# Reordering the end of an expert search, and starting the next search right behind the first index

## The chip, the cores and the metric

One core of a Trainium2 chip. The metric is the device time of one execution in microseconds (us). Engines: PE (TensorE, matmuls and transposes), DVE (VectorE), ACT (ScalarE), POOL (GpSimd), SP (SyncE, which issues DMAs).

## The reference

Causal attention over q, k, v of shape (4, 12, 448, 64), then a mixture of experts over its 1792 output rows of 768 numbers. Each of eight experts takes exactly 224 rows:

```python
logits = x @ w_gate
order = np.argsort(-logits.flatten())
for idx in order:
    tok, e = idx // E, idx % E
    if assigned[tok] >= 0 or counts[e] >= cap:
        continue
    assigned[tok] = e
    counts[e] += 1
for e in range(E):
    h = np.maximum(x[assigned == e] @ w1[e], 0.0)
    out[assigned == e] = h @ w2[e]
```

So the expert that fills up first keeps its 224 best rows; its logits and those rows are then struck out, and the rest goes on.

## The kernel before

**Attention** takes about the first 136 us; its rows go to a table in DRAM (tile xd), the logits stay in tile L: 128 partitions, NB = 14 blocks of tokens, E = 8 experts.

**Searches.** Class Router finds, one after the other, which expert fills up next and which rows it takes. Search p has these steps, each a generator in which `yield "DVE", 0.75` means: what follows runs on DVE, and the planner books 0.75 us for it.

- best (lines 891 to 899; search 0 has early and first in its place): the best logit m, its expert tm and a one-hot A of each row, then integer keys.
- round (901 to 930), five times: compare the keys with thresholds (same, line 824, tile G, on DVE), count them per expert with 14 matmuls (line 929), and pick (932 to 946) a threshold from the counts.
- close (948 to 960): DVE operations most, cw, tx (which expert), then two cuts of the keys. In their midst expert (962 to 964) writes the expert's number ei as an integer, which SP reads to load that expert's weights.
- members (975 to 1018): gq and a scan on DVE (983, 987), two matmuls (990, 991), then pos, slot and val (994 to 998), and one-hots oh of the slots, eight blocks and then six (1004; blocks go in pairs, so slices 0:4 and 4:7); the second half of val (1008) stands between them. Fourteen matmuls (1013) make the index of the rows, a DVE cast (1017) writes it as idx.
- retire (1020 to 1030): cm and acc, which hold minus 1e30 for the expert and for the rows that are gone, are added to L.

**Experts.** For search p's rows: POOL issues two indirect DMAs (gather, line 1336, halves u = 0 and 1) that fetch 112 rows each from xd; PE turns them (1357), ACT copies them (1364), and the first product with w1 follows (first, 1399 for the first half of expert 0, 1403 and 1404 later), then w2 (1432, 1433, 1464). Weights are loaded in eight pieces of 768 KB by SP (fetch, 1312 and 1315); pieces 1 to 3 of expert 0 wait for a copy of ei (ei2, 1340) that POOL makes behind the second gather. The large matmuls take each number as a sum of two, so ACT rounds each piece of weights (1321) and DVE subtracts (1327).

**The order of the work** on each engine is fixed when the program is built. Class Schedule (76 to 159) keeps tasks with durations, priorities and latencies between engines, and always gives the engine that is free first its ready task of highest priority. The steps of a search have 10.9, the first transposes of expert 0 have 13 and the first matmuls 13.5 (1185, 1218). Booked times: gather 1.03 on POOL, then 0.85 until the DMA, 0.96 for it and 1.0 until the rows of half 0 are there (1181, 1182); a transpose step 0.2, its ACT copy 0.27 (1194, 1198). While the flag filling is set, until the first expert matmul, PE's free time is filled with matmuls that nothing reads (filler, 1345).

**What held the second search back.** route (1090 to 1113) chains the searches. After search 0 it sets `self.pace = self.sent`, an event that gather fires for half 1 of expert 0 (1343), with a latency of 1.0. On the chip itself, tile big, which the operation cm reads (1025), is only written by POOL behind the two gathers (1341). The PSUM banks pass from attention to the experts in banks (1071), called from turn (1351).

Of the kernel before, what the change touches and what calls it, by code (L numbers as in the profile page):

```python
# [7 lines left out]
F32 = mybir.dt.float32  # L8
F32R = mybir.dt.float32r
F16 = mybir.dt.float16  # L10
# [4 lines left out]
OP = mybir.AluOpType  # L15
# [4 lines left out]
C, P, NC = 112, 128, 4  # L20
E, CAP = 8, 224
DM, FF = 768, 1024
NB = 14
# [15 lines left out]
BIG = 1.0e30  # L39
# [723 lines left out]
class Router:  # L763
    def __init__(self, nc, cs, k, L):
        self.nc, self.cs, self.k, self.L = nc, cs, k, L

        self.G = cs.tile([P, NB * 128], BF, name="G")
        nc.gpsimd.memset(self.G, 0.0)
        self.oh = cs.tile([P, NB * C + 32], F16, name="oh")
        nc.gpsimd.memset(self.oh[:, NB * C:], 0.0)  # L770
        self.cds, self.turn = {}, 0
        self.big = cs.tile([P, 1], F32, name="big")
        for n in sorted({d.n for ds_ in DIGITS for d in ds_}):
            self.cds[n] = cs.tile([128, 2, E + 1], F16, name=f"cd{n}")
            nc.gpsimd.memset(self.cds[n], 0.0)
# [172 lines left out]
    def close(self):  # L948
        nc, sb, k = self.nc, self.sb, self.k
        yield "DVE", 1.0  # L950
        most = sb.tile([P, 1], F32, name="most")
        nc.vector.tensor_reduce(most, self.nn[:P, :E], axis=AX.X, op=OP.max)
        cw = sb.tile([P, E], F32, name="cw")
        nc.vector.scalar_tensor_tensor(cw, self.nn[:P, :E], most, k["w8"], op0=OP.is_equal, op1=OP.mult)
        self.tx = sb.tile([P, 1], F32, name="tx")
        nc.vector.tensor_reduce(self.tx, cw, axis=AX.X, op=OP.max)
        self.cut = sb.tile([P, 2, NB], F16, name="cut")
        nc.vector.tensor_scalar(self.cut[:, 0], self.kw, most, None, op0=OP.is_gt)
        self.expert()
        nc.vector.tensor_scalar(self.cut[:, 1], self.kw, most, None, op0=OP.is_equal)  # L960

    def expert(self):
# [3 lines left out]
    def last(self):  # L966
        nc, sb = self.nc, self.sb
        yield "DVE", 0.75
        self.m = sb.tile([P, NB], F32, name="m")
        nc.vector.tensor_reduce(self.m, self.L, axis=AX.X, op=OP.max)  # L970
        self.tx = sb.tile([P, 1], F32, name="tx")
        nc.vector.tensor_reduce(self.tx, self.wo, axis=AX.X, op=OP.max)
        self.expert()

    def members(self, last=False):
        nc, sb, k = self.nc, self.sb, self.k
        yield "DVE", 0.5
        gq = sb.tile([P, 2, NB], F16, name="gq")
        if last:
            nc.vector.tensor_scalar(gq[:, 0], self.m, -BIG / 8, None, op0=OP.is_gt)  # L980
            nc.vector.memset(gq[:, 1], 0.0)
        else:
            nc.vector.scalar_tensor_tensor(gq, self.tm[:, None, :].to_broadcast([P, 2, NB]), self.tx, self.cut,
                                           op0=OP.is_equal, op1=OP.mult)
        g2 = gq.rearrange("p s b -> p (s b)")
        run = sb.tile([P, 2 * NB], F16, name="run")
        nc.vector.tensor_tensor_scan(run, k["on"][:P, :2 * NB], g2, LIFT, op0=OP.mult, op1=OP.add)
        yield "PE", 0.06
        p = self.psum()
        nc.tensor.matmul(p[:, 0:2 * NB], k["tri"], g2, start=True, stop=False)  # L990
        nc.tensor.matmul(p[:, 0:2 * NB], k["on"], run, start=False, stop=True)
        yield "DVE", 0.4
        pos = sb.tile([P, NB], F32, name="pos")
        nc.vector.tensor_reduce(pos, p[:, 0:2 * NB].rearrange("p (s b) -> p b s", s=2), axis=AX.X, op=OP.min)
        slot = sb.tile([P, NB], F16, name="slot")
        nc.vector.scalar_tensor_tensor(slot, pos, -1.0, pos, op0=OP.mult, op1=OP.max)
        val = sb.tile([P, NB, 2], F16, name="val")
        nc.vector.scalar_tensor_tensor(val[:, :, 1], pos, 0.0, k["tv"], op0=OP.is_gt, op1=OP.mult)
        oh = self.oh
        hot = oh[:, :NB * C].rearrange("p (b t s) -> p b t s", t=C, s=2)  # L1000
        for s in (slice(0, 4), slice(4, 7)):
            yield "DVE", 0.07 + 0.117 * (s.stop - s.start)
            shape = [P, s.stop - s.start, C, 2]
            nc.vector.tensor_tensor(hot[:, s], k["io"][:, None].to_broadcast(shape),
                                    slot.rearrange("p (b s) -> p b s", s=2)[:, s, None, :].to_broadcast(shape),
                                    op=OP.is_equal)
            if s.start == 0:
                nc.vector.tensor_tensor(val[:, :, 0], k["tv"], val[:, :, 1], op=OP.subtract)
        yield "PE", 0.41
        p = self.psum()  # L1010
        for b in range(NB):
            o = b // 2 * 2 * C
            nc.tensor.matmul(p[:, 0:2], oh[:, o:o + 256].rearrange("p (t s) -> p t s", s=2)[:, :, b % 2], val[:, b],
                             start=b == 0, stop=b == NB - 1)
        yield "DVE", 0.07
        self.idx = sb.tile([C, 2], I32, name="idx", bufs=E)
        nc.vector.tensor_copy(self.idx, p[:C, 0:2])
        self.pos = pos

    def retire(self):  # L1020
        nc, sb, L = self.nc, self.sb, self.L
        b3 = [P, NB, E]
        yield "DVE", 1.05
        cm = sb.tile([P, E], F32, name="cm")
        nc.vector.tensor_scalar(cm, self.k["w8"], self.tx, self.big, op0=OP.is_equal, op1=OP.mult)
        acc = sb.tile([P, NB], F32, name="acc")
        nc.vector.tensor_scalar(acc, self.pos, float(C), -BIG, op0=OP.is_lt, op1=OP.mult)  # L1027
        nc.vector.tensor_tensor(L, L, cm[:, None, :].to_broadcast(b3), op=OP.add)
        nc.vector.tensor_tensor(L, L, acc[:, :, None].to_broadcast(b3), op=OP.add)
        nc.vector.scalar_tensor_tensor(self.wo, self.wo, self.tx, self.wo, op0=OP.not_equal, op1=OP.mult)  # L1030

class Experts(Schedule):
# [57 lines left out]
    def route(self):  # L1090
        rt = self.rt
        for p in range(E):
# [10 lines left out]
                yield from rt.close()  # L1103
            else:
                yield from rt.last()
            self.eis.append(rt.ei)
            self.fire(self.ei[p])
            yield from rt.members(p == E - 1)
            self.idx[p] = rt.idx
            self.fire(self.ix[p])  # L1110
            if p < E - 1:
                self.pace = self.sent if p == 0 else self.pace
                yield from rt.retire()

    def late(self):
        at = self.at
# [216 lines left out]
    def gather(self, p, u):  # L1333
# [4 lines left out]
        if p == 0 and u == 1:  # L1338
            self.ei2 = self.sb.tile([1, 1], I32, name="ei2")
            self.nc.gpsimd.tensor_copy(self.ei2, self.eis[0][0:1])  # L1340
            self.nc.gpsimd.memset(self.rt.big, -BIG)
            self.fire(self.again)
            self.fire(self.sent)

# [196 lines left out]
```

## Time and profile before

| what | value |
|---|---|
| median of 3 runs | 452.05 us (451.25 to 452.68) |
| the profiled execution | 450.93 us |
| its span, first to last instruction | 449.2 us |
| PE busy | 438.9 us (98%) |
| DVE busy | 368.9 us (82%) |
| ACT busy | 295.8 us (66%) |
| POOL busy | 75.1 us (17%) |
| mean granted clock of PE | 0.998 |

All times in the rows below are us from the span's start, in the one profiled execution. The 98% of PE contain the fillers, so they don't say that PE had work everywhere. A merged line such as "x14" gives the start of the first, the time from there to the end of the last, and the count. In brackets stands how long the engine had been idle before, and what released it.

### The profile page before, as it was taken

To read this page: it belongs to the slowest core of one execution; us is meant where nothing else is said; L and a number is where in the kernel's file an instruction comes from. 1 tells how busy PE (TensorE), PEld (TensorE's weight loads), DVE (VectorE), ACT (ScalarE), POOL (GpSimd) and SP (SyncE) were. 2 spreads that over 40 slices of the span, in tenths; PEclk is the share of its full clock that TensorE was granted. 3 is DMA by queue.
4 is the path that set the end of the run, shared out by engine and by line. 5 is a ranking of instruction groups with operands and counts; after the bars stand their busy time and mean duration, and the time that the engine had idled before them with its cause. 6 is when DMAs were issued, how large, how long until landed. Compare 5 with 4: busy or idle time off the path is not lost.

```text
span 449.2 us, 11897 instructions
## 1 busy us (share of the span) xinstructions
PE 438.9 (98%) x4506; PEld 380.6 (85%) x4506; DVE 368.9 (82%) x1246; ACT 295.8 (66%) x733; POOL 75.1 (17%) x192
## 2 busy tenths in 40 slices
PE   7999999999999999999999999999999999999994
PEld 4767676767678899999999999899989999999994
DVE  4998888878889579998999999899999698787400
ACT  6999999999978066556366456556554676865310
POOL 7112132312120201020111103003002500100101
PEclk9999999999999999999999999999999999999999
DMA  7994584560005877776587588378667969871201
GB/s 258 421 387 166 172 341 154 206 271 3 2 1 158 245 261 244 258 217 249 155 266 268 153 268 281 118 237 278 187 196 234 305 210 286 272 231 46 63 15 47
DMA packets 20041, 91.30 MB, mean 203 GB/s; under 512 B 2288, under 2 KB 5392, under 8 KB 18704
## 3 DMA queue, kind: packets, MB, share of 16 engines
q1 hardware_dynamic: 16896, 79.08, 52.5%
q0 software_dynamic: 2608, 11.01, 7.7%
q8 instruction: 35, 0.57, 0.5%
q10 hardware_dynamic: 480, 0.46, 0.3%
q14 instruction: 22, 0.18, 0.1%
HBM read 79.53 MB, written 11.01 MB: 202 GB/s over the span
## 4 chain that ended last, share of the span: by engine, by line
PE 67%; issue 19%; DMA 4%; DVE 4%; POOL 3%; ACT 2%; SPq 0%; POOLq 0%; ACTq 0%
PE po L1464 15%; PE s L245 9%; PE s L323 9%; PE ph L1403 9%; PE s L299 6%; PE ph L1404 4%; DMA wr<-in_w 3%; PE rt L929 2%; PE po L1432 2%; POOL out L1482 2%; PE s L253 1%; PE s L411 1%; DMA raw<-in_qk 1%; PE ph L1357 1%; PE ph L1399 1%
## 5 line engine op out<-in xcount | busy, mean ns | idle before, releaser
L1327 DVE TENSOR_TENSOR wl<-wr,wh 128x512 fp32r<-128x512 f32 x186 | 119.7, 681 | 0.0
L1403 PE MATMUL ph<-xhl,wh 128*128 128x448 f32 x336 | 109.6, 380 | 0.0
L1321 ACT CAST wh<-wr 128x1536 fp32r<-128x1536 f32 x62 | 91.8, 1482 | 18.3 <-DMA wr<-in_w 15.1
L269 ACT ACTIVATE P<-Sm,mx 128x320 f32<-128x320 f32 (+3 forms) x168 | 87.8, 538 | 6.0 <-DVE mx L262 5.5
L1404 PE MATMUL ph<-xhl,wl 128*128 128x224 f32 x336 | 89.2, 265 | 0.0
L1464 PE MATMUL po<-wh,H 128*112 128x384 f32 x320 | 85.4, 342 | 0.0
L1403 PEld LDWEIGHTS ph<-xhl,wh 128*128 128x128 f32 x336 | 63.2, 188 | 5.1 <-issue 0.3
L1404 PEld LDWEIGHTS ph<-xhl,wl 128*128 128x128 f32 x336 | 64.2, 191 | 0.0
L1464 PEld LDWEIGHTS po<-wh,H 128*112 128x112 f32 x320 | 55.0, 175 | 0.3
L1464 PE MATMUL po<-wl,H 128*112 128x384 f32 x160 | 54.7, 342 | 0.0
L245 PE MATMUL s<-raw 64*128 64x320 f32 (+2 forms) x288 | 46.9, 443 | 1.1 <-DMA raw<-in_qk 1.1
L1432 PE MATMUL po<-H,wh 128*128 128x448 f32 x144 | 46.9, 380 | 0.0
L323 PE MATMUL s<-PT,v 128*64 128x64 f32 (+3 forms) x644 | 44.5, 290 | 0.0
L323 PEld LDWEIGHTS s<-PT,v 128*64 128x64 f32 x644 | 31.0, 138 | 12.4 <-issue 8.2
L262 DVE CUSTOM_DVE_ANT_0 Sm<-s,MK 128x320 f32<-128x320 f32 (+2 forms) x72 | 33.2, 486 | 8.9 <-PE s L245 8.4
L1433 PE MATMUL po<-H,wl 128*128 128x224 f32 x144 | 38.3, 266 | 0.0
L1336 POOL DMA_INDIRECT xio<-xd,idx x16 | 17.7, 1104 | 116.8 <-DVE acc L1027 92.0
L1482 POOL DMA_INDIRECT out<-xio,idx x15 | 16.7, 1114 | 121.7 <-ACT xio L1468 62.9
L1409 ACT ACTIVATE H<-hs 128x224 fp32r<-128x224 f32 x60 | 23.4, 392 | 20.1 <-DVE hs L1417 20.0
L1413 ACT COPY hc<-ph 128x224 f32<-128x224 f32 x60 | 20.5, 341 | 23.2 <-PE ph L1404 19.3
L245 PEld LDWEIGHTS s<-raw 64*128 64x128 f32 x288 | 28.6, 187 | 7.6 <-DVE PT L305 2.9
L269 ACT ACTIVATION_READ_ACCUMULATOR P<-Sm,mx 128x1 f32 x168 | 34.6, 206 | 0.0
(212 smaller groups left out, 749.9 us busy)
## 6 DMA issues: line engine op xcount, KB each, us to landing
wr<-in_w SPq DMA_DIRECT2D x64, 768.0 KB, 5.0
raw<-in_qk SPq DMA_DIRECT2D x10, 1024.0 KB, 11.4
v<-in_v SPq DMA_DIRECT2D x11, 896.0 KB, 9.3
xd<-xio SPq DMA_DIRECT2D x2, 1152.0 KB, 5.3
raw<-in_qk SPq DMA_DIRECT2D x3, 512.0 KB, 5.9
xd<-xio SPq DMA_DIRECT2D x3, 384.0 KB, 3.7
v<-in_v SPq DMA_DIRECT2D x2, 448.0 KB, 6.6
xd<-xio SPq DMA_DIRECT2D x3, 192.0 KB, 5.1
```

What stands on the lines that cost most here:

```text
L245: self.nc.tensor.matmul(ts[sd][:, o:o + m], q[:, QS[i]:QS[i] + P], k, start=True, stop=True)
L262: self.nc.vector.tensor_tensor_reduce(Sm[:, QO[i] + sd * m:QO[i] + sd * m + m], self.S.pop((pp, sd, i)), mk, -0.125, 3.0e38, OP.add, OP.mi ...
L269: self.nc.scalar.activation(X[:, s], Sm[:, s], AF.Exp, bias=mx[:, o], scale=-1.0, accum_out=rw[:, o])
L299: self.nc.tensor.transpose(t[z][:, n * 64:n * 64 + 64], X[h, o:o + P], idf[h, h])
L323: self.nc.tensor.matmul(self.AV[pp][sd * 64:sd * 64 + 64, w:w + m], v[:, j if j < 3 else 3 + (3, 2, 0, 1)[j - 3], :], PT[:, o:o + m], star ...
L1321: self.nc.scalar.copy(hi, self.R[p, c])
L1327: self.nc.vector.tensor_sub(lo[:, s], self.R[p, c][:, s], hi[:, s].bitcast(F32))
L1403: nc.tensor.matmul(t[:, :2 * CAP], hi[:, s], x.rearrange("p z t -> p (z t)"), start=d == 0, stop=False)
L1404: nc.tensor.matmul(t[:, :CAP], lo[:, s], x[:, 0], start=False, stop=d == 5)
L1432: self.nc.tensor.matmul(t[:, :2 * CAP], hi[:, o:o + 128], H[:, f].rearrange("p z t -> p (z t)"), start=f == 0, stop=False)
L1433: self.nc.tensor.matmul(t[:, :CAP], lo[:, o:o + 128], H[:, f, 0], start=False, stop=f == 7)
L1464: self.nc.tensor.matmul(self.O[u, z][:, :384], self.H[p][:, f, h, u * C:u * C + C], w[:, o:o + 384], start=f == 0 and n == 0, stop=f == 7 ...
```

## The change

close: the first cut now stands between cw and tx, and ei is gone from there. In search 0, ei is written in members, behind the scan, while DVE would wait for PE (the argument also); in the later searches it is written behind the second cut. members: the one-hots come in ten blocks and four; the first val operation has moved behind the ten, in front of the second one; and cm and acc, which were the first two operations of retire, follow the four. The planner's 1.05 us for retire become 0.75. big is written once at the start of the program. route no longer waits for sent, and calls banks right behind the first index.

```diff
@@ -770,6 +770,7 @@
         nc.gpsimd.memset(self.oh[:, NB * C:], 0.0)
         self.cds, self.turn = {}, 0
         self.big = cs.tile([P, 1], F32, name="big")
+        nc.gpsimd.memset(self.big, -BIG)
         for n in sorted({d.n for ds_ in DIGITS for d in ds_}):
             self.cds[n] = cs.tile([128, 2, E + 1], F16, name=f"cd{n}")
             nc.gpsimd.memset(self.cds[n], 0.0)
@@ -952,11 +953,10 @@
         nc.vector.tensor_reduce(most, self.nn[:P, :E], axis=AX.X, op=OP.max)
         cw = sb.tile([P, E], F32, name="cw")
         nc.vector.scalar_tensor_tensor(cw, self.nn[:P, :E], most, k["w8"], op0=OP.is_equal, op1=OP.mult)
+        self.cut = sb.tile([P, 2, NB], F16, name="cut")
+        nc.vector.tensor_scalar(self.cut[:, 0], self.kw, most, None, op0=OP.is_gt)
         self.tx = sb.tile([P, 1], F32, name="tx")
         nc.vector.tensor_reduce(self.tx, cw, axis=AX.X, op=OP.max)
-        self.cut = sb.tile([P, 2, NB], F16, name="cut")
-        nc.vector.tensor_scalar(self.cut[:, 0], self.kw, most, None, op0=OP.is_gt)
-        self.expert()
         nc.vector.tensor_scalar(self.cut[:, 1], self.kw, most, None, op0=OP.is_equal)
 
     def expert(self):
@@ -970,9 +970,8 @@
         nc.vector.tensor_reduce(self.m, self.L, axis=AX.X, op=OP.max)
         self.tx = sb.tile([P, 1], F32, name="tx")
         nc.vector.tensor_reduce(self.tx, self.wo, axis=AX.X, op=OP.max)
-        self.expert()
-
-    def members(self, last=False):
+
+    def members(self, last=False, also=None):
         nc, sb, k = self.nc, self.sb, self.k
         yield "DVE", 0.5
         gq = sb.tile([P, 2, NB], F16, name="gq")
@@ -985,6 +984,8 @@
         g2 = gq.rearrange("p s b -> p (s b)")
         run = sb.tile([P, 2 * NB], F16, name="run")
         nc.vector.tensor_tensor_scan(run, k["on"][:P, :2 * NB], g2, LIFT, op0=OP.mult, op1=OP.add)
+        if also:
+            also()
         yield "PE", 0.06
         p = self.psum()
         nc.tensor.matmul(p[:, 0:2 * NB], k["tri"], g2, start=True, stop=False)
@@ -995,17 +996,22 @@
         slot = sb.tile([P, NB], F16, name="slot")
         nc.vector.scalar_tensor_tensor(slot, pos, -1.0, pos, op0=OP.mult, op1=OP.max)
         val = sb.tile([P, NB, 2], F16, name="val")
-        nc.vector.scalar_tensor_tensor(val[:, :, 1], pos, 0.0, k["tv"], op0=OP.is_gt, op1=OP.mult)
         oh = self.oh
         hot = oh[:, :NB * C].rearrange("p (b t s) -> p b t s", t=C, s=2)
-        for s in (slice(0, 4), slice(4, 7)):
+        for s in (slice(0, 5), slice(5, 7)):
             yield "DVE", 0.07 + 0.117 * (s.stop - s.start)
             shape = [P, s.stop - s.start, C, 2]
             nc.vector.tensor_tensor(hot[:, s], k["io"][:, None].to_broadcast(shape),
                                     slot.rearrange("p (b s) -> p b s", s=2)[:, s, None, :].to_broadcast(shape),
                                     op=OP.is_equal)
             if s.start == 0:
+                nc.vector.scalar_tensor_tensor(val[:, :, 1], pos, 0.0, k["tv"], op0=OP.is_gt, op1=OP.mult)
                 nc.vector.tensor_tensor(val[:, :, 0], k["tv"], val[:, :, 1], op=OP.subtract)
+        if not last:
+            self.cm = sb.tile([P, E], F32, name="cm")
+            nc.vector.tensor_scalar(self.cm, k["w8"], self.tx, self.big, op0=OP.is_equal, op1=OP.mult)
+            self.acc = sb.tile([P, NB], F32, name="acc")
+            nc.vector.tensor_scalar(self.acc, pos, float(C), -BIG, op0=OP.is_lt, op1=OP.mult)
         yield "PE", 0.41
         p = self.psum()
         for b in range(NB):
@@ -1020,11 +1026,8 @@
     def retire(self):
         nc, sb, L = self.nc, self.sb, self.L
         b3 = [P, NB, E]
-        yield "DVE", 1.05
-        cm = sb.tile([P, E], F32, name="cm")
-        nc.vector.tensor_scalar(cm, self.k["w8"], self.tx, self.big, op0=OP.is_equal, op1=OP.mult)
-        acc = sb.tile([P, NB], F32, name="acc")
-        nc.vector.tensor_scalar(acc, self.pos, float(C), -BIG, op0=OP.is_lt, op1=OP.mult)
+        yield "DVE", 0.75
+        cm, acc = self.cm, self.acc
         nc.vector.tensor_tensor(L, L, cm[:, None, :].to_broadcast(b3), op=OP.add)
         nc.vector.tensor_tensor(L, L, acc[:, :, None].to_broadcast(b3), op=OP.add)
         nc.vector.scalar_tensor_tensor(self.wo, self.wo, self.tx, self.wo, op0=OP.not_equal, op1=OP.mult)
@@ -1103,14 +1106,20 @@
                 yield from rt.close()
             else:
                 yield from rt.last()
-            self.eis.append(rt.ei)
-            self.fire(self.ei[p])
-            yield from rt.members(p == E - 1)
+            if p:
+                self.chosen(p)
+            yield from rt.members(p == E - 1, None if p else lambda: self.chosen(0))
             self.idx[p] = rt.idx
             self.fire(self.ix[p])
             if p < E - 1:
-                self.pace = self.sent if p == 0 else self.pace
+                if p == 0:
+                    self.banks()
                 yield from rt.retire()
+
+    def chosen(self, p):
+        self.rt.expert()
+        self.eis.append(self.rt.ei)
+        self.fire(self.ei[p])
 
     def late(self):
         at = self.at
@@ -1338,7 +1347,6 @@
         if p == 0 and u == 1:
             self.ei2 = self.sb.tile([1, 1], I32, name="ei2")
             self.nc.gpsimd.tensor_copy(self.ei2, self.eis[0][0:1])
-            self.nc.gpsimd.memset(self.rt.big, -BIG)
             self.fire(self.again)
             self.fire(self.sent)
```

## Rows read from the trace of the kernel before

**Rows 1.** Busy time by stage: stretch, length, each engine's us, PE clock, DMA share, GB/s.

```profile
156.00:170.00 14.00, 13.93 (x147) 12.97 (x146) 11.57 (x41) 9.01 (x16) 0.00 (x0) 1.00 0.71 238
```

**Rows 2.** PE's waits from 150 us on: us in total, times, longest.

```profile
PE ph L1357 <- DMA xio<-xd,idx: 0.7, 1, 0.7
PE ph L1357 <- DVE hs L1417: 0.4, 1, 0.4
PE rt L929 <- DVE G L824: 0.3, 1, 0.3
PE rt L946 <- DVE cd L943: 0.3, 1, 0.3
```

**Rows 3.** Order of time on PE, from the first index to the first expert matmuls.

```profile
150.22 0.60 PE L1013 MATMUL s<-val,oh 128*128 128x2 f16 x14
150.69 4.23 PE L1347 MATMUL s<-on 128*112 128x256 f16 x37
155.57 0.77 PE L1357 MATMUL ph<-idf,xio 112*128 112x112 f32 x6 [0.66 <-DMA xio<-xd,idx]
156.18 0.28 PE L1347 MATMUL po<-on 128*112 128x256 f16 x1
156.44 2.04 PE L1399 MATMUL po<-xhl,wr 128*128 128x112 f32 x16
```

**Rows 4.** Order of time on DVE, at the end of the first search.

```profile
147.30 0.23 DVE L954 SCALAR_TENSOR_TENSOR cw<-s,most,w 128x8 f32<-128x8 f32 x1
147.56 0.16 DVE L956 TENSOR_REDUCE tx<-cw 128x1 f32<-128x8 f32 x1
147.64 0.23 DVE L958 TENSOR_SCALAR cut<-kw,most 128x14 f16<-128x14 f32 x1
147.77 0.15 DVE L964 TENSOR_SCALAR ei<-tx 128x1 int32<-128x1 f32 x1
147.83 0.23 DVE L960 TENSOR_SCALAR cut<-kw,most 128x14 f16<-128x14 f32 x1
...
149.08 0.17 DVE L996 SCALAR_TENSOR_TENSOR slot<-pos 128x14 f16<-128x14 f32 x1
149.17 0.17 DVE L998 SCALAR_TENSOR_TENSOR val<-pos,tv 128x14 f16<-128x14 f32 x1
149.29 0.62 DVE L1004 TENSOR_TENSOR oh<-io,slot 128x896 f16<-128x896 f16 x1
149.83 0.17 DVE L1008 TENSOR_TENSOR val<-tv,val 128x14 f16<-128x14 f16 x1
149.92 0.50 DVE L1004 TENSOR_TENSOR oh<-io,slot 128x672 f16<-128x672 f16 x1
150.86 0.16 DVE L1017 CAST idx<-s 112x2 int32<-112x2 f32 x1 [0.45 <-PE s L1013]
```

**Rows 5.** Order of time on DVE, at the beginning of the second search.

```profile
154.03 0.29 DVE L1025 TENSOR_SCALAR cm<-w,tx,big 128x8 f32<-128x8 f32 x1 [3.00 <-POOL xio L1331]
...
154.35 0.28 DVE L1028 TENSOR_TENSOR L<-L,cm 128x112 f32<-128x112 f32 x1
...
157.25 1.16 DVE L824 TENSOR_TENSOR G<-kr,kk 128x1024 bf16<-128x1024 int16 x2
```

**Rows 6.** The chain that ended last: one count of a round, 14 matmuls.

```profile
163.77 0.33 PE rt L929 x14
```

**Rows 7.** Busy time by stage, columns as in rows 1, while the first weights land.

```profile
152.00:153.00 1.00, 1.00 (x11) 1.00 (x10) 0.00 (x0) 0.00 (x0) 0.69 (x2) 1.00 0.93 389
153.00:154.00 1.00, 1.00 (x12) 1.00 (x11) 0.00 (x0) 0.00 (x0) 0.99 (x4) 1.00 0.80 184
```

**Rows 8.** Order of time on POOL: three of the sixteen gathers.

```profile
151.32 1.19 POOL L1336 DMA_INDIRECT xio<-xd,idx  x1 [5.56 <-DVE idx L1017]
...
309.67 0.93 POOL L1336 DMA_INDIRECT xio<-xd,idx  x1 [29.34 <-DVE acc L1027]
...
347.06 2.94 POOL L1336 DMA_INDIRECT xio<-xd,idx  x1 [4.64 <-DVE idx L1017]
```

## The prediction

> **What bounds the kernel now.** I read three views in this order: the busy time by stage, what TensorE (PE) waited for, and the order of time on PE, VectorE (DVE) and GpSimd (POOL) around the first gather. From 156 us on, PE is the bound: in the first stage of the experts it is busy 13.93 of 14.00 us at a granted clock of 1.00 [rows 1]. Over the whole rest of the program its own waits, after the one for the first gathered rows, are three, together 1.0 us [rows 2]. So two things only can move the end: when PE's real work begins, and how much PE work lies behind that beginning.
>
> It begins like this [rows 3]. The 14 index matmuls of the first search start at 150.22. Then PE has nothing to do but 37 filler matmuls and a wait of 0.66 us, until the first gathered rows have landed at 155.57. Six transposes, one filler, and at 156.44 the first expert matmul. Between 150.8 and 155.57, PE time is free; behind 156.44 it is not.
>
> **The end of the first search** [rows 4]. The reader is to see two kinds of spacing: an operation that reads the result of the one before starts about 0.21 us after it (slot 149.08, one-hots 149.29), one that doesn't starts 0.09 to 0.13 us after it, although each lasts about 0.17 us (val 149.83, one-hots 149.92).
>
> *Closing step.* cw to tx is a dependent pair, 0.26 us apart, and the first cut takes 0.13 us of DVE (147.64 to 147.77), so put between them it fits into the wait: 0.13 us saved. The expert number ei (147.77 to 147.83) leaves the path: 0.06 us saved. I take 0.18 together. ei now runs behind the scan, where DVE waits for PE anyway. The lower bound is 0.06, if the cut does not fit.
>
> *One-hots.* Before, from the first one-hot operation to the end of the second: 0.54 + 0.09 + 0.50 = 1.13 us. The one-hots cost 0.12 us for every two blocks (0.62 for eight, 0.50 for six, as durations), so ten blocks hold DVE 0.67 us, and four last 0.38. The first val operation stood in the shadow of slot and cost nothing there, as the 0.21 us from slot to one-hots is the dependent spacing. Now it stands behind the ten blocks, directly in front of the second val operation, which reads it: 0.21, then 0.09 to the four blocks. After: 0.67 + 0.21 + 0.09 + 0.38 = 1.35, so 0.22 us later. In return four index matmuls instead of six are left behind the last one-hot. Fourteen last 0.60 us, of which one alone is 0.17, so 0.033 each: 0.07 saved. Net 0.15 us lost; 0.03 if the pair of val operations needs only 0.09.
>
> By this the index comes 0.18 - 0.15 = 0.03 us earlier; ends 0.15 earlier and 0.09 later. The Trainium skill (VectorE: DVE Perf Modes, The DRAIN you can't avoid) says that the next operation does not start until the pipe of the one before is empty. By that rule moving the cut and val would be neutral and ei worth its full 0.15 us; with the 0.07 of PE the index would come 0.22 us earlier, and the sum below would be -0.43. The trace disagrees, since starts 0.09 us apart overlap operations of 0.17.
>
> The two operations cm and acc come in behind the four blocks: 154.03 to 154.35 is 0.32 us of DVE [rows 5]. They run while PE does the last index matmuls; that cover is about 0.45 us, the wait in front of idx [rows 4], so nothing. Without it they would cost up to 0.32. In the six later searches all this is DVE time beside a busy PE: nothing. The memset of big moves to POOL's start, some 150 us ahead of its first reader: nothing; behind the two gathers it stood on POOL in front of nothing that PE waits for.
>
> **The second search** [rows 5]. DVE sat idle 3.00 us until POOL had issued both gathers, then ran from 154.35 (L, with cm and acc done) to the first one-sided compare at 157.25, two of them, 1.16 us: ready at 158.41, or 4.06 us after 154.35. After the change L starts right behind idx, at about 150.9, so the compare is ready at about 154.95, before the gathered rows. Its 14 count matmuls take 0.33 us in the chain [rows 6]. They lay behind 156.44; now they can lie in front of it. Where does the planner put them? In its own times after the index: retire 0.75, best 2.2, compares 0.67 and 0.52, latency 0.16: ready at 4.31. The transposes become ready at 0.2 + 1.03 + 0.85 + 0.96 + 1.0 = 4.04 and hold PE for three times 0.2, to 4.64; the first expert matmul needs an ACT copy and is ready at 4.84. At 4.64 only the count is ready, so it goes there, into the slot in which one filler stood, 156.18 to 156.44 = 0.26 us [rows 3]. The count is 0.07 longer than the slot, so 0.33 - 0.07 = 0.26 us gained. Ends: 0.33, and 0 if the planner puts it later. One count only: the next needs the pick and two more compares, and by then expert matmuls with a higher priority are ready. The other rounds come some 3 us earlier, but cost PE the same.
>
> **What is late next: the weights.** ei leaves 147.77 and starts behind the second cut (147.83, less the 0.18 saved), two dependent steps of about 0.26 (gq, scan) and a free one of 0.13 [rows 4]: at about 148.3, so the load of the first weights is issued some 0.55 us later on SP. Behind it on SP stand only the loads that wait for the gathers. Its bytes ran at 389 GB/s in 152 to 153 us, and in the next us the engines still show 0.80 busy at 184 GB/s [rows 7]. Moved by 0.55 us, up to 0.55 x 0.389 = 0.21 MB of it falls on the gather's packets, which can start at 152.51 when its issue ends [rows 8]. The bound above is full serialisation, 0.55 us; below it is nothing, as that stretch has (389 - 184) x 1 us = 0.2 MB to spare. I take 0.05, near the row with room. The weights themselves were through by about 154 [rows 7]; 0.55 us later is still ahead of 156.44.
>
> **Sum.** -0.03 (index) - 0.26 (count) + 0.05 (weights) = -0.24 us. The profiled run took 450.93 (span 449.2), so 450.7; the median of the runs is 452.05, 1.12 above it, and becomes 451.8. That is 0.05%. 0.3% is 1.36 us, about what a measurement of this kernel can tell from no change.
>
> **Rivals.**
>
> *The planner or the chip keeps the count behind the first expert matmuls* (the change does not do what it says). Then -0.03 + 0.05: 452.1. For it: the slot is narrow, 4.64 against 4.84. Against: the times above. Chance 0.14.
>
> *The late weights hold up the first gather in full.* -0.03 - 0.26 + 0.55 = +0.26: 452.3. For it: the engines are 0.93 and 0.80 busy. Against: the room in 153 to 154. Chance 0.10.
>
> *DVE beside the gather slows it* (slower). The wait that is removed kept DVE idle while POOL wrote the first two gathers. The slowest gather of the run, with DVE at work beside it, took 2.94 us, where the first one takes 1.19 with DVE idle [rows 8]: +1.75, and -0.24 for the rest gives 453.6. It decides as soon as the gather loses more than 1.6 us, the 0.24 won and 1.36 together. Against: the gather at 309.67 ran beside the very operations that now come here (retire and best) in 0.93 us [rows 8]. Chance 0.06. The Trainium skill (SBUF — State Buffer, Who interferes with whom) says that tensor_scalar operations in a two-port mode lock GpSimd out of the port through which it writes descriptors. That would be this rival; the 0.93 us speaks against it here, the 2.94 for something like it.
>
> *Order behind the beginning gets better too.* The order of the whole rest is planned anew; if the three waits of 1.0 us [rows 2] go and the index gains its 0.15, -0.15 - 0.33 - 1.0 = -1.5: 450.6. Nothing shows why they should go. Chance 0.08.
>
> **How the numbers follow.** The forecast has 0.62. Its own range is the terms' ends, -0.48 to +0.3, and the spread of the runs (451.25 to 452.68, some 0.7 about the median), which also moves the result: 450.8 to 452.8 leaves out most of the slower rival and the far half of the last one. Faster than 0.3%: the last rival and a little of the spread, 0.10. Slower: the third rival and a little, 0.07. Within: 0.83.
>
> **What would show it.** Right: idx starts within 0.15 us of 150.86; the gather is issued within 0.15 of 151.32 and lasts under 1.3; L starts at about 150.9 with no idle DVE before; the first 14 counts of the second search stand between the transposes and the first expert matmul, and none between 156.5 and 159; from there to the end everything is shifted by 0.2 to 0.3 us and PE's later waits stay near 1.0 us. Wrong: the gather lasts 1.9 us or more, or its rows land later than 155.6 (weights); the one-hots end before 150.4 (val does not wait); or the later waits of PE change by more than 0.5 us, so that the new order, not the beginning, makes the time.

## The result and the profile after

| | before | after |
|---|---|---|
| median of 16 runs | 451.89 us (451.25 to 454.19) | 454.22 us (452.34 to 457.71) |
| profiled execution, its span | 450.93, 449.2 us | 453.14, 451.4 us |
| mean granted clock there | 0.998 | 0.999 |

The ratio is 1.0055 (95% interval 1.0041 to 1.0069): slower by 2.3 us, outside the range that was given. The runs also spread more widely than those of before.

**The beginning.** PE in order of time, as [rows 3] (lines have moved: fillers L1355, members L991, index L1019, transposes L1365, counts L930, first product L1407):

```profile
147.56 1.82 PE L1355 MATMUL s<-on 128*112 128x256 f16 x15
149.22 0.18 PE L991 MATMUL s<-gq,tri 128*128 128x28 f16 x1
...
156.43 0.79 PE L1365 MATMUL ph<-idf,xio 112*128 112x112 f32 x6 [0.36 <-DMA xio<-xd,idx]
157.06 0.50 PE L930 MATMUL rt<-A,G 128*128 128x8 bf16 x14
157.42 0.79 PE L1407 MATMUL po<-xhl,wr 128*128 128x112 f32 x5
```

DVE in order of time, as [rows 4, 5]:

```profile
147.94 0.23 DVE L955 SCALAR_TENSOR_TENSOR cw<-s,most,w 128x8 f32<-128x8 f32 x1
...
148.55 0.25 DVE L982 SCALAR_TENSOR_TENSOR gq<-tm,tx,cut 128x28 f16<-128x28 f32 x1
...
149.49 0.18 DVE L995 TENSOR_REDUCE pos<-s 128x14 f32<-128x28 f32 x1 [0.40 <-PE s L992]
149.71 0.17 DVE L997 SCALAR_TENSOR_TENSOR slot<-pos 128x14 f16<-128x14 f32 x1
149.92 0.74 DVE L1004 TENSOR_TENSOR oh<-io,slot 128x1120 f16<-128x1120 f16 x1
150.58 0.17 DVE L1008 SCALAR_TENSOR_TENSOR val<-pos,tv 128x14 f16<-128x14 f32 x1
150.78 0.18 DVE L1009 TENSOR_TENSOR val<-tv,val 128x14 f16<-128x14 f16 x1
150.87 0.39 DVE L1004 TENSOR_TENSOR oh<-io,slot 128x448 f16<-128x448 f16 x1
...
151.66 0.16 DVE L1023 CAST idx<-s 112x2 int32<-112x2 f32 x1
151.73 0.26 DVE L1031 TENSOR_TENSOR L<-L,cm 128x112 f32<-128x112 f32 x1
```

The reader is to see the change doing what it says: the first val operation stands behind ten blocks, L follows idx without a pause, and the first count stands between the transposes and the first product. Everything in this execution stands 0.64 us later than in [rows 3, 4] already ahead of the change (cw at 147.94, not 147.30). That is the execution, not the kernel: in the traces of the first four runs below the shift at the same place is 0.20 to 1.13 us, and one of them (e4) has the code of before up to there.

**The rest.** PE's waits from 150 us on, as [rows 2]: us in total, times, longest.

```profile
PE rt L947 <- DVE cd L944: 1.7, 2, 1.4
PE ph L1365 <- DVE hs L1425: 0.4, 1, 0.4
PE ph L1365 <- DMA xio<-xd,idx: 0.4, 1, 0.4
PE po L1355 <- DVE idx L1023: 0.2, 1, 0.2
```

The wait for the first rows has shrunk (0.4 for 0.7), and one group has grown: L947, the matmul of pick in a later search, waits for DVE. I laid the starts of the 1560 expert products of both traces side by side, the n-th against the n-th. The first transpose comes 0.86 us later than before (0.64 of it the shift above), the first product 0.98, number 120 only 0.52 (the count that is no longer in the way: a gain, as forecast), and then PE loses: from number 160 to 240 (185 to 203 us) 0.74, from 640 to 680 (280 to 288 us) 1.24. From there on the distance stays within 0.4 us and ends at 2.20. So without the shift the beginning stands 0.12 us ahead at number 120, and all the loss lies behind it.

The larger loss, read in the timeline of all engines (the number in brackets is how long the engine had been idle):

```profile
285.29 1.48 ACT L1330 CAST wh<-wr 128x1536 fp32r<-128x1536 f32 x1 [1.32 <-DMA wr<-in_w]
286.68 0.38 ACT L1417 ACTIVATE H<-hs 128x224 fp32r<-128x224 f32 x1
...
287.09 0.39 DVE L1429 SCALAR_TENSOR_TENSOR H<-hs,H 128x224 fp32r<-128x224 f32 x1 [1.21 <-ACT H L1417]
...
287.70 0.16 DVE L944 TENSOR_SCALAR_CACHE_REDUCE cd<-rt 128x8 f16<-128x8 f32 x1
...
287.92 0.16 PE L947 MATMUL rt<-cd,on 128*128 128x1 f16 x1 [1.41 <-DVE cd L944]
```

Read upward: PE waits for the pick; the pick stands on DVE behind H (what rounding leaves of the hidden layer) and hs (the next sum of a first product); H waits for ACT's relu; the relu stands behind L1330, the rounding of a piece of weights whose DMA is late. Every queue is in order, so one late load reaches PE, over two engines that have nothing to do with it. It is the 32nd rounding of the program. Before, the planner had put the 32nd behind the last relus of the layer, where ACT did not wait for it (no bracket):

```profile
291.80 1.50 ACT L1321 CAST wh<-wr 128x1536 fp32r<-128x1536 f32 x1
```

### The profile page after: what moved, and what is told of

It is laid out like the page before. It is cut to its first block, busy times and chain, and to the rows that moved or that the text cites. A ratio compares the mean times of both kernels' runs of the same rounds, so it can differ in the third digit from the quotient of the medians.

```text
span 451.4 us, 11896 instructions
## 1 busy us (share of the span) xinstructions
PE 440.8 (98%) x4505; PEld 382.0 (85%) x4505; DVE 368.6 (82%) x1246; ACT 295.5 (65%) x733; POOL 75.8 (17%) x192
## 4 chain that ended last, share of the span: by engine, by line
PE 68%; issue 14%; DMA 6%; DVE 5%; ACT 4%; POOL 2%; POOLq 0%; SPq 0%; ACTq 0%; DVEq 0%
PE po L1472 13%; PE ph L1411 10%; PE s L245 9%; PE s L323 9%; PE s L299 5%; PE ph L1412 5%; DMA wr<-in_w 5%; PE po L1440 3%; PE rt L930 2%; DVE wl L1336 2%; ACT P L269 2%; PE ph L1365 2%; PE po L1441 1%; POOL out L1490 1%; PE po L1407 1%
## 5 line engine op out<-in xcount | busy, mean ns | idle before, releaser
L1330 ACT CAST wh<-wr 128x1536 fp32r<-128x1536 f32 x62 | 91.7, 1481 | 24.8 <-DMA wr<-in_w 23.1
L245 PE MATMUL s<-raw 64*128 64x320 f32 (+2 forms) x288 | 48.0, 451 | 0.0
L1345 POOL DMA_INDIRECT xio<-xd,idx x16 | 18.8, 1176 | 114.1 <-DVE L L1031 100.5
L262 DVE CUSTOM_DVE_ANT_0 Sm<-s,MR 128x320 f32<-128x320 f32 (+2 forms) x72 | 31.5, 486 | 0.0
```

What stands on the lines that cost most here:

```text
L245: self.nc.tensor.matmul(ts[sd][:, o:o + m], q[:, QS[i]:QS[i] + P], k, start=True, stop=True)
L262: self.nc.vector.tensor_tensor_reduce(Sm[:, QO[i] + sd * m:QO[i] + sd * m + m], self.S.pop((pp, sd, i)), mk, -0.125, 3.0e38, OP.add, OP.mi ...
L1330: self.nc.scalar.copy(hi, self.R[p, c])
```

## The experiments

Theory A: the loss sits in the new order behind the beginning. Rival B: the beginning decides. Rival C: the later start of attention. The kernel before ran beside each group: median 452.60 us (35 runs), 452.17 (30) and 452.01 (35).

**e1_early_only.** The kernel before, with the second search started early and nothing else.

```diff
         self.big = cs.tile([P, 1], F32, name="big")
+        nc.gpsimd.memset(self.big, -BIG)
...
-                self.pace = self.sent if p == 0 else self.pace
+                if p == 0:
+                    self.banks()
...
-            self.nc.gpsimd.memset(self.rt.big, -BIG)
```

> The kernel before, with the early second search alone (no wait for sent, banks behind the first index, big written at the start); close, one-hots, cm and acc stay as before. Theory A (the loss is in the order planned anew: a search step that DVE reaches late, behind a weight piece that lands late, holds PE): the first count of the second search moves in front of the first expert matmul and the first layer of expert 0 ends 0.3 to 0.5 us earlier than before, but the end can lie anywhere from -0.5 to +2.5 us, and its distance from that gain is found as longer waits of PE for search steps. Rival B (the loss is in the beginning: index, gather, first count): the end follows the beginning, 451.5. Rival C (the changed program starts attention 0.6 us later): +0.6 in attention here too, since the memset stands at the start.

451.99 us, ratio 0.9984 (0.9970 to 0.9998). This half of the change, taken alone, is slightly faster; the loss is not in it. Between A and B this run can't decide: A allowed anything from -0.5 to +2.5, and B's -0.4 us is as near.

**e2_end_only.** The changed kernel with the wait for sent put back.

```diff
-                if p == 0:
-                    self.banks()
+                self.pace = self.sent if p == 0 else self.pace
```

> The changed kernel with the wait for sent put back (and banks where it was); close, one-hots, cm and acc as changed. Theory A: the index comes 0.15 to 0.2 us later against the start of the closing step, the first product 0.2 to 0.3 later than before, and the end again anywhere from 0 to +3 us, told by the waits of PE for search steps. Rival B: +0.2 to +0.3 at the end, 452.2. Rival C: +0.6 from attention.

453.04 us, ratio 1.0010 (0.9998 to 1.0021). The two halves alone give -0.0016 and +0.0010, together +0.0055: they don't add, which costs of single instructions would. Taken alone, this run fits A's 0 to +3 us and B's +0.2 to +0.3.

**e3_book_105.** The changed kernel; only a booked time differs, so only the order.

```diff
-        yield "DVE", 0.75
+        yield "DVE", 1.05
```

> The changed kernel with 1.05 us booked for retire in the plan instead of 0.75; no instruction differs, only their order on the engines behind the first index. Theory A: the beginning is that of the changed kernel (first product the same within 0.1 us), yet the end differs from 454.2 by more than 0.5 us, either way, and the waits of PE for search steps differ by the same. Rival B and rival C: 454.2 as the changed kernel, within 0.3.

453.88 us, ratio 1.0027 (1.0011 to 1.0043). By the ratios that is 1.3 us below the changed kernel; the two intervals just touch. The same instructions, another order, most likely another time, as A said. Its waits for picks are 1.0 us (longest 0.5), but two others come in, 0.8 for a compare and 0.5 for a one-hot.

**e4_before_replanned.** The kernel before, planned anew with best booked longer.

```diff
-        yield "DVE", 2.2
+        yield "DVE", 2.3
```

> The kernel before with 2.3 us booked for best instead of 2.2; no instruction differs, only the order planned behind the first index. It measures what a new order alone does. Theory A: the end moves by 0.5 to 2.5 us, more likely up, though the beginning is the same. Rival B and rival C: 451.9, within 0.3.

452.22 us, ratio 0.9989 (0.9976 to 1.0003). A's forecast for it, 0.5 to 2.5 us and more likely up, missed: a new order alone need not cost anything. Rival C falls here: this execution's attention ran 0.58 us later than in the trace of before, without any edit there, and e1, with the memset at the start, ran 0.86 later and is not slower.

**e5_swap_one.** The decisive one: the changed kernel, the 32nd rounding moved behind the relu and the copy that followed it on ACT. All other engines keep their order.

```diff
     def split_hi(self, p, c):
+        self.nth = getattr(self, "nth", -1) + 1
+        if self.nth == 31:
+            self.kept = (p, c)
+            return
+        self.round_piece(p, c)
+
+    def round_piece(self, p, c):
...
     def mid_copy(self, p, f):
...
+        if getattr(self, "kept", None):
+            self.round_piece(*self.kept)
+            self.kept = None
```

> The kernel after the change, but with one instruction moved on ACT: the 32nd rounding of a weight piece (at 285.3 us of the changed kernel's trace, where it sat idle 1.32 us for its DMA) goes behind the relu and the copy that followed it. Every other engine keeps its order, instruction by instruction. Theory A (the loss sits in the new order: a late weight piece holds ACT, that holds DVE, and PE stands at a search's pick): the wait of 1.41 us in front of that pick goes, the longest wait of PE for a pick falls below 0.6 us, and the time is about 1.2 us less than the changed kernel's on the same chip (run beside it here). Rival B (the beginning decides, the wait at 285 us is filled up later anyway): the same time as the changed kernel, within 0.4 us.

452.19 us, ratio 1.0002 (0.9988 to 1.0017), beside 455.07 of the changed kernel in the same group (e8 below). One instruction, moved past two others, gives 2.9 us. In its trace (lines moved by 3 to 13; the pick's matmul is L950) PE's waits are:

```profile
PE ph L1375 <- DVE hs L1438: 1.0, 2, 0.6
PE rt L950 <- DVE cd L947: 0.6, 1, 0.6
```

The wait at 286 us is gone and the one near 190 is left. Part of the gain comes back as a second wait for hs (0.55 us at 290.7): from product 640 to 720 this trace needs 0.76 us less than the first one of the changed kernel, and 3.03 less than the one of e8. Rival B falls. The forecast of A, 1.2 us, was too small; e8 shows why.

**e8_after_again.** The changed kernel, unchanged.

> The changed kernel once more, unchanged, on the chip of these runs. Theory A: about 454.2 us, ratio near 1.005; its PE again loses over 1 us at picks of the second to fourth search, but since it hangs on when weight pieces land, the size of the single waits differs from the first trace and the runs spread more widely (over 2 us) than those of e5_swap_one and e6_end_same_plan. Rival B: the waits are the same as in the first trace to 0.1 us.

455.07 us (453.70 to 456.82), ratio 1.0065 (1.0041 to 1.0089). The same two rows:

```profile
286.28 1.47 ACT L1330 CAST wh<-wr 128x1536 fp32r<-128x1536 f32 x1 [2.34 <-DMA wr<-in_w]
...
288.90 0.16 PE L947 MATMUL rt<-cd,on 128*128 128x1 f16 x1 [2.42 <-DVE cd L944]
```

The piece was issued at the same time (278.62; 278.65 in the first trace) and landed 1.0 us later, and PE's wait is longer by just that. Then the clock. Busy time by us (PE, PEld, DVE, ACT, POOL, then granted clock, DMA share, GB/s):

```profile
286.00:287.00 1.00, 0.48 (x4) 0.30 (x3) 0.00 (x0) 0.72 (x1) 0.00 (x0) 1.00 0.12 46
287.00:288.00 1.00, 0.00 (x0) 0.00 (x0) 0.00 (x0) 1.00 (x3) 0.00 (x0) 1.00 0.01 3
288.00:289.00 1.00, 0.10 (x2) 0.10 (x1) 0.93 (x5) 0.47 (x3) 0.00 (x0) 1.00 0.00 0
...
291.00:292.00 1.00, 1.00 (x5) 0.93 (x4) 1.00 (x4) 0.28 (x1) 0.00 (x0) 0.50 0.66 227
```

One us of full work later PE was granted 0.50, its lower level of 1.2 GHz, from 290 to 293 us, and from the start of product 680 to that of 720 it took 10.34 us instead of 9.08. In the first trace, after a wait of 1.41 us, the clock stayed at 1.00. So a late piece costs PE 1.4 us in one execution and 2.4 + 1.25 = 3.7 in another; against the kernel before, whose two waits of 0.3 us [rows 2] lie there too, it is 0.9 and 3.2 from product 640 to 720. That goes with the wide spread of this kernel's runs, whose two slowest (of 16) show a mean clock of 0.989.

**e6_end_same_plan.** All instructions of the changed kernel, with the booked times of before, so that the planner makes e1's order.

```diff
-        for s in (slice(0, 5), slice(5, 7)):
-            yield "DVE", 0.07 + 0.117 * (s.stop - s.start)
+        for s, n in ((slice(0, 5), 4), (slice(5, 7), 3)):
+            yield "DVE", 0.07 + 0.117 * n
...
-        yield "DVE", 0.75
+        yield "DVE", 1.05
...
             if p:
                 self.chosen(p)
+            self.fire(self.ei[p])
...
         self.eis.append(self.rt.ei)
-        self.fire(self.ei[p])
```

> All instructions of the changed kernel, but booked with the times of before (one-hots as if eight and six, retire 1.05, the expert's number announced at the end of close), so that the planner makes the very order of e1_early_only, on PE and on every other engine, but for the moved instructions themselves. Theory A: the same time as e1_early_only within 0.5 us, 451.6 to 452.5, faster than the changed kernel by about 2 us, although it executes the same instructions. Rival D (the reordered end costs by itself: later one-hots in each of the eight searches, cm and acc in front of the cast): slower than e1_early_only by 1 us or more, 453 or above.

452.59 us, ratio 1.0009 (0.9994 to 1.0023): 2.5 us below the changed kernel beside it, with the very same instructions. So the order makes most of the loss. The time lies between A's 452.5 and D's 453. By the ratios it stands 0.0025, or 1.1 us, above e1, which is D's size, but the two intervals overlap and the groups differ: a cost of the reordered end by itself is suggested, not shown. In the traces e6 falls 1.4 us behind e1, half of it in the second search. First e1, then e6:

```profile
176.37 0.16 DVE L1018 CAST idx<-rt 112x2 int32<-112x2 f32 x1
...
178.06 0.93 POOL L1338 DMA_INDIRECT xio<-xd,idx  x1 [0.31 <-issue]
...
178.91 0.34 SPq L1317 DMA_DIRECT2D wr<-in_w  x1
...
184.69 1.48 ACT L1323 CAST wh<-wr 128x1536 fp32r<-128x1536 f32 x1 [3.44 <-DMA wr<-in_w]
```

```profile
176.78 0.15 DVE L1023 CAST idx<-rt 112x2 int32<-112x2 f32 x1
...
178.56 1.00 POOL L1345 DMA_INDIRECT xio<-xd,idx  x1 [0.31 <-issue]
...
178.89 0.34 SPq L1324 DMA_DIRECT2D wr<-in_w  x1
...
187.05 1.48 ACT L1330 CAST wh<-wr 128x1536 fp32r<-128x1536 f32 x1 [5.86 <-DMA wr<-in_w]
...
190.67 0.16 PE L947 MATMUL rt<-cd,on 128*128 128x1 f16 x1 [0.48 <-DVE cd L944]
```

The index is 0.41 us later (0.27 of it cm and acc, now ahead of the cast), so the second gather is issued 0.5 us later against the same weight load. In e1 most of the gathers' bytes move first; in e6 they are mixed with the load's (0.31 MB of the gathers in 182 to 184 us, against 0.06), and the piece takes 8.16 us from its issue to the rounding instead of 5.78. This repeats: with the second gather issued 0.3 us ahead of the load it takes 7.67 to 8.31 us in six traces (the changed kernel's two, e3, e5, e6, e12), with 0.85 us 5.78 to 6.07 in three (e1, e7, e9). The rest is the known chain: ACT's copies of the turned rows behind the rounding, DVE, pick, PE.

**e9_end_first_only.** e6 with the reordered end in the first search alone (marks writes cm and acc, in the later searches at the head of retire again).

```diff
+        if not also:
+            nc.vector.scalar_tensor_tensor(val[:, :, 1], pos, 0.0, k["tv"], op0=OP.is_gt, op1=OP.mult)
-        for s, n in ((slice(0, 5), 4), (slice(5, 7), 3)):
+        at = 5 if also else 4
+        for s, n in ((slice(0, at), 4), (slice(at, 7), 3)):
...
-        if not last:
...
+        if also:
+            self.marks(pos)
...
     def retire(self):
...
+        if not self.first_search:
+            self.marks(self.pos)
```

> e6_end_same_plan with the reordered end in the first search alone: in the seven later ones the one-hots are eight and six again, val stands ahead of them, and cm and acc follow the index; the planned order is that of e1_early_only and e6_end_same_plan. Theory E (in the second search of e6_end_same_plan the index cast stands 0.41 us later on DVE than in e1_early_only, 176.78 against 176.37, of which cm and acc in front of it are 0.27; so the second gather is issued behind the weight load of 178.9, that piece lands 2.4 us later, its rounding holds ACT, ACT holds DVE, DVE the pick): the index comes at about 176.3, the rounding that waited until 187.05 starts before 185.2, the wait of PE for the pick near 190.7 (0.48) goes, and the time is that of e1_early_only: ratio 0.997 to 0.9995. Rival F (e6 differed from e1 by the execution only): rounding at 187 and a wait at the pick again, ratio near 1.001.

The trace does what E says, but the index comes at 176.68, 0.4 us later than forecast, since PE loses 0.4 us against e1 at a count and a pick between 167 and 169:

```profile
178.38 0.94 POOL L1356 DMA_INDIRECT xio<-xd,idx  x1 [0.31 <-issue]
...
179.23 0.34 SPq L1335 DMA_DIRECT2D wr<-in_w  x1
...
185.30 1.48 ACT L1341 CAST wh<-wr 128x1536 fp32r<-128x1536 f32 x1 [3.73 <-DMA wr<-in_w]
```

The wait for the pick near 190 is gone. The time is 452.23 us, ratio 1.0008 (0.9990 to 1.0025), which is F's number, though the trace is E's: what the later index costs over many runs isn't resolved.

**e10_swap_two.** e5 with the 7th rounding also moved, behind the three copies of the turned rows.

```diff
-        if self.nth == 31:
+        if self.nth in (6, 31):
...
+    def let_go(self):
+        if getattr(self, "kept", None):
+            self.round_piece(*self.kept)
+            self.kept = None
...
     def turn_hi(self, p, d, us):
...
+        if self.nth == 6 and d == 2:
+            self.let_go()
```

> e5_swap_one with a second rounding moved on ACT: the 7th (at 186.9 us, where ACT sat idle 5.1 us for its DMA) goes behind the first eviction and the three copies of the turned rows that followed it. PE, DVE and POOL keep the order of the changed kernel. Theory A: the wait for the pick near 190 (0.3 to 0.8 us of PE in the traces of this order) goes, from 185 to 200 us PE loses 0.5 to 0.8 us less, and the time is so much below e5_swap_one: 451.4 to 451.8, ratio 0.9985 or below. Rival B: as e5_swap_one, ratio 0.9995 to 1.001.

The wait near 190 is gone, and from product 160 to 240 PE takes 16.89 us instead of 17.83 in e5. That is about A's forecast for the stretch; 0.42 of it is lost again between 640 and 720, and the whole doesn't follow: 451.96 us, ratio 0.9996 (0.9980 to 1.0012), which can't be told from e5, as rival B said.

**e7_close_fewer_fill.** e1 with the new close and without the last four of the fifteen fillers ahead of the members matmuls; e11 (below) leaves out the same four.

```diff
     def filler(self):
+        self.fills = getattr(self, "fills", 0) + 1
+        if 37 <= self.fills <= 40:
+            return
```

> e1_early_only with the new order of close alone (first cut between cw and tx, the expert's number behind the scan), with the one-hots and cm, acc as before, and with the last four of the fifteen fillers in front of the first members matmul left out; the planned order is that of e1_early_only. My reading that the saving in close was eaten by those fillers: from most to idx 3.76 us in e1_early_only becomes 3.50 to 3.60, the members matmuls wait for the scan and no longer stand behind fillers, and the first expert matmul comes as much earlier; time about 451.8, not to be told from e1_early_only. Rival (something else than the fillers held the members matmuls): 3.70 or more.

451.40 us, ratio 0.9978 (0.9961 to 0.9995): beside e1 the only version whose interval lies below the kernel before; from e1 it can't be told. From most to idx it takes 3.57 us, as expected; the members matmul comes 1.32 us after the pick's (147.48), and pos waits for the scan's matmul:

```profile
148.80 0.17 PE L991 MATMUL s<-gq,tri 128*128 128x28 f16 x1
...
149.26 0.18 DVE L995 TENSOR_REDUCE pos<-s 128x14 f32<-128x28 f32 x1 [0.22 <-PE s L992]
```

**e11_swap_short_end.** e10 with one-hots eight and six, cm and acc behind the index, and the four fillers out.

```diff
-        for s in (slice(0, 5), slice(5, 7)):
-            yield "DVE", 0.07 + 0.117 * (s.stop - s.start)
+        for s, n in ((slice(0, 4), 5), (slice(4, 7), 2)):
+            yield "DVE", 0.07 + 0.117 * n
```

> e10_swap_two with three parts of the change in the end of a search undone or mended, in the same planned order: one-hots eight and six with val ahead of them, cm and acc behind the index again (in every search), and the last four of the fifteen fillers in front of the first members matmul left out. The order of close, the early second search and the two moved roundings stay. Theory A with the fillers: the first index comes 0.3 to 0.4 us earlier than in e10_swap_two (0.15 one-hots, 0.2 fillers), the time is about 0.4 us below it: 451.0 to 451.4, ratio near 0.9975, below the kernel before and the changed one. Rival (the order has other weak places that then show): no faster than e10_swap_two.

451.72 us, ratio 0.9996 (0.9980 to 1.0012). From most to idx 3.57 us against 3.92 in e10: the 0.35 is there. In the time it can't be seen; the rival's forecast (no faster than e10) came.

**e12_weights_booked_late.** The changed kernel, with the latency of weight pieces from the fifth on booked as 4.0 us instead of 2.5.

```diff
-(0.95, 0.95, 3.6, 1.6)[g] if g < 4 else 2.5, 1.1)
+(0.95, 0.95, 3.6, 1.6)[g] if g < 4 else 4.0, 1.1)
```

> The changed kernel with one booked time altered: weight pieces from the fifth on are booked as there 4.0 us after their load instead of 2.5, nearer to what the traces show; the planner makes a new order of it, whose planned end is 0.6 us later (310.96 against 310.34). Theory A (the cause is that the planner places roundings ahead of what PE needs sooner, at times when the piece is not there yet): ACT's waits for weight pieces from 150 us on fall from 23 us to under 12, no wait of PE for a pick is over 0.6 us, and the time is 452 to 453.5, below the changed kernel by 1 us or more. Rival (any new order is as good or bad as another, the booking of the weights doesn't matter): anywhere from 452 to 455, with ACT's waits for weights unchanged.

451.63 us, ratio 0.9999 (0.9982 to 1.0016). Waits from 150 us on, of ACT for weights in the changed kernel:

```profile
ACT wh L1330 <- DMA wr<-in_w: 23.1, 16, 5.1
```

and in e12, of ACT and of PE:

```profile
ACT wh L1330 <- DMA wr<-in_w: 12.1, 9, 3.6
...
PE rt L947 <- DVE cd L944: 0.6, 3, 0.2
```

The time came out below A's 452 to 453.5, the waits as forecast but for 0.1 us. One booked number takes the loss away without touching an instruction. That it was this number, and not just a new order, is argued: the orders of e3 and e4, made with other bookings, cost 0.0027 and nothing. It was booked as 2.19 + 2.5 = 4.7 us from the load's start to the piece, which the 32nd piece took 6.6 us (278.65 to 285.29) and 7.7 us to reach.

## Why the prediction was wrong

The median was forecast 0.25 us below the one shown, and is 2.3 above that of before. Step by step:

- *Closing step, -0.18.* Right: cw to gq takes 0.61 us (147.94 to 148.55), 0.80 in e1, which has the old order (148.16 to 148.96). The 0.15 that the prediction took from the Trainium skill (VectorE: DVE Perf Modes, The DRAIN you can't avoid) is less near, but not by enough to settle it. The same section of the Trainium skill adds that a next operation that is not held starts earlier; the trace agrees, as one-hots start 0.09 us after a val operation of 0.18 (150.78, 150.87), so the two don't differ here, though the prediction took them to.
- *It did not reach the index.* This I had missed: the fifteen fillers ahead of L991 are laid out by booked times, which did not change. From the pick's matmul to the members matmul (L942 and L991, before L941 and L990) it is 1.69 us before (146.89 to 148.58) and after (147.53 to 149.22). e7, without four of them, brings the gain back.
- *One-hots, +0.15.* Right: slot to idx is 1.95 us, 1.78 in [rows 4]: +0.17. Index in all +0.16 (cw to idx 3.72 against 3.56), forecast -0.03.
- *The count in the slot, -0.26.* Right in kind and about in size: [rows 6]'s 14 matmuls stand ahead of the first product, and from the first transpose to product 120, with five counts in both kernels, PE takes 22.20 us instead of 22.54, 0.34 less.
- *Late weights, +0.05.* Right in the number, by luck. From the gather's issue to the first transpose it is 4.31 us, 4.25 in [rows 3, 8], but these 0.06 are the gather's own (1.25 us for 1.19): from its end on it is 3.06 in both. And the load is not 0.55 us late: it comes 0.85 us later than before, 0.64 of which is the shift, so 0.21, as SP's read of ei takes 0.48 us instead of 0.80. The gather comes 0.80 later, so load and gather keep their distance to 0.05 us. The rival with 0.55 did not come, and was not tested: its delay never arose. Before, then after:

```profile
149.40 0.37 SPq L1315 DMA_DIRECT2D wr<-in_w  x1
...
150.25 0.38 SPq L1324 DMA_DIRECT2D wr<-in_w  x1
```

- *DVE beside the gather.* Falls: 1.25 us beside L, wo and best, 1.19 in [rows 8]. The rule of the Trainium skill (SBUF — State Buffer, Who interferes with whom) that I had weighed is about tensor_scalar operations in a two-port mode. Such operations (the keys, 153.77 to 154.4; in which mode, no trace shows) stand beside the second gather alone, and it took 1.00 us, 0.95 before with DVE idle: no lock shows itself.

```profile
152.12 1.25 POOL L1345 DMA_INDIRECT xio<-xd,idx  x1 [5.73 <-DVE L L1031]
153.67 1.00 POOL L1345 DMA_INDIRECT xio<-xd,idx  x1 [0.30 <-issue]
```

- **The step that failed** is "The other rounds come some 3 us earlier, but cost PE the same", and beside it "Order behind the beginning gets better too". The prediction knew that the whole rest is planned anew, and asked only whether the 1.0 us of waits in [rows 2] would go. It never priced the other side: that the new order puts an instruction that waits for a DMA ahead of one that PE is about to need. The trace of before held what was wanted, ACT's waits for weight pieces (15.1 us in 14 waits from 150 us on; 23.1 in 16 after). They are harmless as long as nothing urgent stands behind them: e5 has 21.6 us of them and no loss. The signpost given, later waits of PE that change by more than 0.5 us, is what came: without those for the first index and the first rows, 1.0 us in [rows 2] became 2.1 (L947 1.7, hs 0.4). The largest of it is the 1.41 us behind the 32nd rounding, 2.42 in e8. ACT's waits in the trace of before (us in total, times, longest):

```profile
ACT wh L1321 <- DMA wr<-in_w: 15.1, 14, 2.5
```

- "In the six later searches all this is DVE time beside a busy PE: nothing" failed in the trace: the second index came 0.41 us later and the gather ran into a weight load (e6 against e1). In the time of many runs this is unresolved (e9).

Shown: the 32nd rounding (e5, e8), and that bookings alone decide it (e6, e12). Not separated by a run of its own: how much of the changed kernel's median is the wait and how much the clock behind it. The runs on record give a hint: of its 16, the seven with a mean clock of 0.998 or more have a median of 453.29 us, the other nine 454.80, while the same split of the 30 runs of before beside e8 gives 452.17 and 452.16. By that some 1.4 of the 2.3 us would be there without the clock.

## What to carry to other kernels

Where a planner fixes the order from booked times, a local edit is priced twice: by its own instructions, and by what the new order puts at the head of each in-order queue; look on every engine for instructions that wait for a DMA and ask who stands behind them. Book transfers by the landing times of the trace: here 1.5 us more on one booked number took the whole loss away, though another new order might have done so too. Time saved ahead of booked fillers does not reach the next step until they are cut, and even then the end need not show it (e11).

## What the runs showed of the hardware

- A wait of 2.42 us, with PE busy 0.58 us in three, was followed by three us at 0.50 of the clock, which cost 1.25 us more; a wait of 1.41 us was not.
- A load of 768 KB issued at the same time to 0.03 us landed 1.0 us apart in two executions of one program.
- A gather that comes 0.5 us later against a weight load cost that load 2.4 us (8.16 for 5.78; 7.67 to 8.31 in six traces, 5.78 to 6.07 in three): far more than it was late.
